# A transformer block on one core: a third value pair by Strassen, the exp and the statistics passes of a group moved, numerators in four row tiles, and the first loads from two queues

## The chip, the cores and the metric

The kernel runs on one core of a Trainium2 chip. The metric is the device time of one launch in microseconds (us), as the median of several executions. Each trace is of one execution.

Engine names are those of the profile: PE is TensorE's matmuls, PEld its weight loads, DVE is VectorE, ACT is ScalarE, POOL is GpSimd, SP is SyncE, which issues most DMAs.

## The reference, cut to what matters

```python
def reference(A_x, A_wqkv, A_wo, B_x, B_W_gate, B_W_up, B_W_down):   # S = 2048, D = 1024, H = 32, Dh = 32, F = 3584
    # A: linear attention on layernorm(x)
    qkv = layernorm(x) @ wqkv                        # q, k, v: 32 heads of 32
    phi = lambda t: where(t > 0, t + 1, exp(t)) + 1e-6
    kv  = einsum("bhsd,bhse->bhde", phi(k), v)       # one 32x32 block a head
    z   = einsum("bhsd->bhd", phi(k))
    o   = einsum("bhqd,bhde->bhqe", phi(q), kv) / (einsum("bhqd,bhd->bhq", phi(q), z) + 1e-6)
    h   = x + o @ wo
    # B: gated block on layernorm(h)
    out = h + (relu(g @ W_gate) * (g @ W_up)) @ W_down      # g = layernorm(h)
```

## The kernel before

The 2048 rows are 16 tiles of 128 rows, numbered from 0. The first stage goes through them in pairs (tiles 4 and 5 are the third pair), a group of key products and a group of value products for each pair; then come eight query groups, the output projection, and the gated block. A group is one level of Strassen's scheme: seven products of four 128x128x512 matmuls instead of eight. The order of the products is P1, P7, P6, P2, P5, P4, P3, and between them ScalarE copies a bank of PSUM, TensorE's output memory, into the next one (`fk1`, `fk2`), evacuates partial sums (`s7`, `sc`), and runs the exp of phi; VectorE adds and finishes phi. A hook is a place between two products where work of another stage is queued.

```python
def sgroup(...):                              # one group; hook(i) runs what other stages put there
    prod(a, X(0, 0), W(0, 0), True, "P1")
    ident_act(bank(b), bank(a), ..., "fk1")   # ScalarE; P6 waits for it
    hook(1)
    prod(f, SX(2), TW(2), True, "P7")         # SX: sums of x blocks (VectorE), TW: sums of weight blocks
    ident_act(s7, bank(f), ..., "s7")
    hook(2)
    prod(b, SX(1), TW(1), False, "P6")
    ident_act(bank(c), bank(b), ..., "fk2")   # P5 waits for it
    hook(3)
    prod(a, X(1, 0), W(1, 0), False, "P2"); ...; hook(4)
    prod(c, SX(0), TW(0), False, "P5")
    ident_act(sc, bank(c), ..., "sc"); s22 = ...; s22[0]()
    hook(5)
    prod(b, X(1, 1), TW(3), False, "P4"); s21 = ...; s21[0](); hook(6)
    prod(c, SX(3), W(1, 1), False, "P3")
    s12 = list(e12(...))
    if isq: s12.pop(0)()                      # exp; the other exps wait until hooks 1 to 3 of the next group
    pend[1], pend[2], pend[3] = s12, list(s22[1:]), list(s21[1:])
    hook(7)
```

The statistics of half of the tiles are made on ScalarE (a mean pass and a square pass over 1024 columns), in hooks 5 and 6 of a key group. The first two value pairs and the third (tiles 4 and 5) are plain products, `v_piece`, because x sums and weight sums come late at the start. The numerators take, for each tile, eight matmuls of 128 rows against a zero-padded kv block, which VectorE makes with a mask:

```python
    for g in range(NG):                                    # 8 groups of 4 heads
        mm(ps[:, nbk, c0:c0 + P + HPG], pqT[:, r, t, g, i * P:(i + 1) * P], kvz[:, g, 0:P + HPG], ...)   # 132 columns
```

A last part is how a normalised tile becomes a transposed one. VectorE normalises, SP issues a transposing DMA from SBUF to SBUF (`T1d`), and VectorE then makes the sums of x blocks (`x_sums`) that P7, P6, P5 and P3 of the groups of that pair need.

## Time and profile before

The time before is 747.6 us (747.31 to 748.15 in three executions). The first lines are from the page of the profile: its span, the busy time of each engine (share of the span, number of instructions), the DMA queue of PE's instruction fetches (packets, MB, share), and the shares of the chain of waits.

```profile
span 746.0 us, 10031 instructions
PE 736.1 (99%) x3539; PEld 336.0 (45%) x3595; DVE 536.7 (72%) x1071; ACT 309.7 (42%) x536; POOL 43.9 (6%) x90
...
q8 instruction: 28, 0.46, 0.3%
...
PE 88%; DVE 5%; ACT 4%; issue 2%; DMA 0%; SPq 0%; DVEq 0%; POOL 0%; ACTq 0%; POOLq 0%
```

TensorE is the limit. A reader should not take "99% busy" for "no loss", though: a 512-column matmul is drawn 379 ns long while the next one starts 216 ns after it, so a wait of 0.1 us hides under the overlap. Losses are read from the distance of starts.

The timeline of the kernel before, around the start of a value group (start, duration, engine, line, operation; `ps<-RW,RWG` at 57.95 is P7 and P6, four matmuls each, `RAB` P2, the next `RW,RWG` P5):

```profile
57.08 1.03 PE L616 MATMUL ps<-RAB 128*128 128x512 bf16 x4
57.22 1.06 ACT L659 ACTIVATE RXH<-RE 128x1024 bf16<-128x1024 bf16 x1
57.95 2.00 PE L616 MATMUL ps<-RW,RWG 128*128 128x512 f16 x8
58.27 0.58 ACT L621 ACTIVATE ps<-ps 128x512 f32<-128x512 f32 x1
59.78 1.03 PE L616 MATMUL ps<-RAB 128*128 128x512 bf16 x4
60.26 0.59 ACT L621 ACTIVATE ps<-ps 128x512 f32<-128x512 f32 x1
60.91 1.04 PE L616 MATMUL ps<-RW,RWG 128*128 128x512 f16 x4
```

P1 is issued at 57.08 and over by about 57.95, but its copy `fk1` starts at 58.27, behind the square pass of the statistics (57.22), and `fk2` at 60.26, behind two exps. P5 starts 1.13 us after P2 (60.91 less 59.78), where four matmuls need 0.86 us. A key-and-value pair takes 13.56 us and holds 0.48 us of such waits.

The numerators of one tile, between P4 and P3 of a query group:

```profile
149.51 1.03 PE L616 MATMUL ps<-RAB,RXH 128*128 128x512 bf16 x4
150.38 0.63 PE L616 MATMUL ps<-kvz,RAB 128*128 128x132 bf16 x8
150.85 1.02 PE L616 MATMUL ps<-RH,RO 128*128 128x512 f16 x4
```

Eight numerator matmuls take 0.47 us from start to start.

### The profile page before, as it was taken

The numbers are of one execution on the slowest core, as the hardware profiler recorded it, in microseconds if no ns is written. First come the engines' busy times: TensorE is split into PE (matmuls) and PEld (weight loads), VectorE is DVE, ScalarE is ACT, GpSimd is POOL, SyncE is SP. The second block draws the span as 40 slices with busy tenths as digits, with TensorE's granted clock in tenths as the row PEclk, the third lists the DMA queues.
The fourth block names the chain that finished last, engine by engine and source line by source line (L and its number), as shares of the span: only waits on it lengthen the run. The fifth ranks groups of instructions, "written<-read, shape, count | busy, mean of one in ns | idle before, by whom it ended". The sixth has DMA issues, their size and how long they took to land.

```text
span 746.0 us, 10031 instructions
## 1 busy us (share of the span) xinstructions
PE 736.1 (99%) x3539; PEld 336.0 (45%) x3595; DVE 536.7 (72%) x1071; ACT 309.7 (42%) x536; POOL 43.9 (6%) x90
## 2 busy tenths in 40 slices
PE   9999999999999999999999999999999999999998
PEld 4444444344554444444444444444444444444443
DVE  7788866898775899787877585766867677563343
ACT  4767656665832354544543100035444454520000
POOL 2411000001350000000000010000000000000000
PEclk9999999999999999999999999999999999999999
DMA  9642144023998797666428899742324242036764
GB/s 305 202 103 68 35 135 156 1 29 84 230 223 248 222 278 210 179 176 171 142 85 253 231 254 305 240 121 77 110 61 112 58 113 56 1 85 184 211 189 135
DMA packets 160226, 113.38 MB, mean 152 GB/s; under 512 B 51505, under 2 KB 141361, under 8 KB 160177
## 3 DMA queue, kind: packets, MB, share of 16 engines
q1 hardware_dynamic: 160176, 112.75, 54.1%
q8 instruction: 28, 0.46, 0.3%
q14 instruction: 22, 0.17, 0.1%
HBM read 85.46 MB, written 15.73 MB: 136 GB/s over the span
## 4 chain that ended last, share of the span: by engine, by line
PE 88%; DVE 5%; ACT 4%; issue 2%; DMA 0%; SPq 0%; DVEq 0%; POOL 0%; ACTq 0%; POOLq 0%
PE ps L616 88%; DVE RAB L691 1%; ACT ps L621 1%; ACT RX L684 1%; DVE RE L1058 1%; DVE RX L688 1%; ACT RXH L654 1%; ACT RXH L659 1%; ACT RX L621 1%; DVE RX L903 0%; DMA RW<-in_B_W_down_dram 0%; SPq L522 0%; DVE RXH L1082 0%; PE ps L748 0%; DVE RE L691 0%
## 5 line engine op out<-in xcount | busy, mean ns | idle before, releaser
L621 ACT ACTIVATE ps<-ps 128x512 f32<-128x512 f32 x154 | 89.8, 584 | 180.2 <-PE ps L616 161.5
L616 PE MATMUL ps<-RC,RO 128*128 128x512 f16 x672 | 154.4, 379 | 0.5 <-DVE RE L1239 0.4
L616 PE MATMUL ps<-RW,RAB 128*128 128x512 f16 (+1 forms) x681 | 150.1, 379 | 0.6
L616 PEld LDWEIGHTS ps<-RW,RAB 128*128 128x128 bf16 (+1 forms) x692 | 67.7, 98 | 81.6
L616 PE MATMUL ps<-RH,RWG 128*128 128x512 bf16 x435 | 103.2, 379 | 1.0 <-DVE RAB L1232 0.3
L621 ACT ACTIVATE RE<-ps 128x512 f32<-128x512 f32 x120 | 70.8, 597 | 75.3 <-PE ps L616 52.8
L616 PEld LDWEIGHTS ps<-RC,RO 128*128 128x128 f16 x672 | 65.5, 98 | 80.5 <-ACT ps L621 1.1
L616 PE MATMUL ps<-RC,RWG 128*128 128x512 f16 x320 | 76.6, 379 | 0.1
L616 PEld LDWEIGHTS ps<-RH,RWG 128*128 128x128 bf16 x448 | 43.8, 98 | 53.4 <-DVE RAB L1232 0.8
L1232 DVE TENSOR_TENSOR RAB<-ps,RAB 128x512 bf16<-128x512 f32 x28 | 19.3, 690 | 63.6 <-PE ps L616 63.6
L621 ACT ACTIVATE RAB<-ps 128x512 bf16<-128x512 f32 x56 | 33.4, 597 | 61.9 <-PE ps L616 61.8
L616 PE MATMUL ps<-RH,RO 128*128 128x512 bf16 (+1 forms) x242 | 58.3, 379 | 0.7
L616 PE MATMUL ps<-RW,RE 128*128 128x512 bf16 x248 | 56.8, 379 | 0.8 <-DVE RXH L1082 0.4
L616 PE MATMUL ps<-RAB 128*128 128x512 bf16 x196 | 47.7, 379 | 0.3
L616 PEld LDWEIGHTS ps<-RC,RWG 128*128 128x128 bf16 (+1 forms) x320 | 30.0, 98 | 39.9 <-ACT ps L621 5.9
L1163 DVE TENSOR_TENSOR RO<-RWG,RO 128x512 f16<-128x512 bf16 x108 | 45.4, 420 | 1.8
L1163 DVE TENSOR_TENSOR RO<-RWG 128x512 f16<-128x512 bf16 x108 | 40.7, 418 | 3.2 <-DMA RWG<-in_B_W_up_dram 1.6
L1239 DVE TENSOR_TENSOR RE<-ps,RE 128x512 f32<-128x512 f32 x56 | 38.3, 690 | 4.9 <-ACT RE L621 4.9
L1244 DVE TENSOR_TENSOR RE<-ps,RE 128x512 f32<-128x512 f32 x56 | 38.1, 681 | 0.0
L616 PEld LDWEIGHTS ps<-RH,RO 128*128 128x128 f16 (+1 forms) x256 | 24.6, 98 | 29.4 <-ACT RX L621 1.1
L616 PEld LDWEIGHTS ps<-RW,RE 128*128 128x128 bf16 x256 | 24.5, 98 | 27.9 <-DVE RXH L1082 0.7
L688 DVE TENSOR_SCALAR RX<-RX 128x512 bf16<-128x512 bf16 x64 | 18.6, 290 | 22.8 <-ACT RX L684 22.7
(118 smaller groups left out, 764.8 us busy)
## 6 DMA issues: line engine op xcount, KB each, us to landing
RWG<-in_B_W_gate_dram SPq DMA_DIRECT2D x28, 512.0 KB, 4.0
RWG<-in_B_W_up_dram SPq DMA_DIRECT2D x28, 512.0 KB, 5.1
RW<-t_scr SPq DMA_DIRECT2D x56, 256.0 KB, 3.3
RW<-in_B_W_down_dram SPq DMA_DIRECT2D x42, 256.0 KB, 4.0
RW<-in_B_W_down_dram SPq DMA_DIRECT2D x14, 512.0 KB, 4.1
t_scr<-RW SPq DMA_DIRECT2D x14, 512.0 KB, 5.0
RE<-in_A_x_dram SPq DMA_DIRECT2D x23, 256.0 KB, 3.2
RAB<-in_A_wqkv_dram SPq DMA_DIRECT2D x8, 512.0 KB, 8.0
```

Of the source, the lines that this page charges most:

```text
L616: lambda e: e.matmul(out_ap, lhsT, rhs, start=start, stop=stop, skip_group_check=skip),
L621: PL.add("act", lambda e: e.activation(out=dst, in_=src, func=func), reads=reads, writes=writes, name=name)
L654: PL.add("act", lambda e: e.activation(out=junk, in_=src, func=ACTF.Identity, scale=1.0 / D, accum_out=sv[:, 0:1]), reads=src_bufs, writes ...
L659: PL.add("act", lambda e: e.activation(out=junk, in_=src, func=ACTF.Square, scale=float(D) ** -0.5, accum_out=sv[:, 1:2]), reads=src_bufs, ...
L684: PL.add("act", lambda e: e.activation(out=Et[:, k, :], in_=src, func=ACTF.Exp), reads=[src_buf], writes=[B_E[k]], name=name + "_exp")
L688: PL.add("dve", lambda e: e.tensor_scalar(out=Et[:, k, :], in0=Et[:, k, :], scalar1=1.0, scalar2=1e-6, op0=ALU.min, op1=ALU.add), reads=[] ...
L691: PL.add("dve", lambda e: e.scalar_tensor_tensor(out=dst_ap, in0=src, scalar=C1, in1=Et[:, k, :], op0=ALU.add, op1=ALU.max), reads=[src_bu ...
L1058: PL.add("dve", lambda e: e.tensor_tensor(out=osb[:, k, :].rearrange("p (g h e) -> p g h e", h=HPG, e=Dh), in0=nv[:, :, 0:P].rearrange("p ...
L1163: PL.add(eng, lambda e: e.tensor_tensor(out=Tring[:, k, j], in0=in0, in1=in1, op=ALU.subtract), reads=reads, writes=[B_T[k][j]], name="T%d ...
L1232: PL.add("dve", lambda e: e.tensor_tensor(out=hh[:, f1, 0:SBW], in0=bank(BA[1]), in1=r11[:, rr, :], op=ALU.mult), reads=[B_bank[BA[1]], B_ ...
L1239: PL.add("dve", lambda e, w=w: e.tensor_tensor(out=ftmp[:, 4 + w, :], in0=bank(BF_[w]), in1=ftmp[:, 2 + w, :], op=ALU.add), reads=[B_bank[ ...
L1244: PL.add("dve", lambda e, w=w: e.tensor_tensor(out=ftmp[:, 6 + w, :], in0=bank(BB[w]), in1=ftmp[:, w, :], op=ALU.add), reads=[B_bank[BB[w] ...
```

## The change

Its intent is to fill the last bubbles of the first 233 us: (1) the third value pair also by Strassen, 28 matmuls for 32; (2) at the end of a group one exp goes before P3's evacuation and one before the next group's `fk1`, and the square pass is cut in two halves placed between other work; (3) numerators of 32 rows x 33 columns, four row tiles of the array at once (a row tile is a band of 32 of TensorE's 128 rows, one for each head of a group; it is not one of the 16 tiles of x), so that the kv blocks need no zero padding and no masks (ten small ScalarE copies bring them from PSUM); (4) the first x tile and the first weights from two DMA queues. The core of the diff:

```diff
-        if isq:
+        for f_ in s22[1:2]:            # before P3: the exp of the P5 result
+            f_()
+        prod(c, SX(3), W(1, 1), False, "P3")
+        s12 = list(e12(bank(c), B_bank[c]))
+        if isphi:
             s12.pop(0)()
-        pend[1] = s12
-        pend[2] = list(s22[1:])
-        pend[3] = list(s21[1:])
+        pend[1] = list(s22[2:]) + s12 + list(s21[1:])
 ...
-        v_piece(4, 0, lambda: run_pend(1))
-        v_piece(4, 1, lambda: run_pend(3))      # and v_piece(5, 0), v_piece(5, 1)
+        v_group(p + 2, {2: v2, 3: v3, 5: v5, 6: v6})      # for p = 0 as for all others
 ...
-            if 3 <= p + 2 < NP_:                # hook 6
-                x_sums(p + 2)
+            if p + 2 < NP_:                     # hook 5: one sum, hook 6: the other three
+                x_sums(p + 2, 0)
 ...
+                for h in range(HPG):            # numerators
+                    sl = slice(h * Dh, (h + 1) * Dh)
+                    mm(ps[:, NB[h], g * NUW:g * NUW + Dh + 1], pqT[sl, r, t, g, i * P:(i + 1) * P],
+                       kvz[sl, g, 0:Dh + 1], ...)
 ...
+                if r == 0 and ct >= 1:          # ten ScalarE copies of the kv blocks
+                    for h_ in (1, 3, 4, 7):
+                        if kvc:
+                            hooks[h_] = kvc.pop(0)
 ...
-                dma(..., writes=[B_x1[i][c]])                        # first x tile, two halves
+                dma(..., writes=[B_x1[i][c]], eng=("sp", "act")[c])
```

## The prediction

> **What bounds the kernel.** TensorE: the page gives PE 736.1 us busy of a 746.0 us span, and 88% of the chain of waits. The gated block (from about 233 us) is untouched, so all happens before. The timeline of PE shows 512-column matmuls starting 0.216 us apart, eight 132-column numerator matmuls in 0.47 us (150.38 to 150.85), sixteen 129-column ones in 0.94 us. From 8.26 to 233.3 us there are 940 of 512 columns (202.8 us), 256 short ones (15 us) and three transposed tiles (1.4 us): 219 us of 225. So some 6 us of bubbles, and 8.3 us before the first projection matmul.
>
> **Terms.**
>
> 1. Third value pair: 32 matmuls become 28. Minus 4 x 0.216 = 0.9 us, all on the chain.
>
> 2. Group boundaries. Each steady key-and-value pair (50.24 to 63.80, 13.56 us) holds about 0.48 us of waits: 0.26 and 0.10 us in the value group, 0.03 to 0.05 elsewhere. The timeline shows ScalarE running the mean and square passes (1.06 us each plus 0.19) just before the value group's bank copies (58.27, 60.26), so P6 waits. Halving the square pass between copies, and putting a group's first exp (0.6 us) inside the last product, removes the queue. Such waits: 3.2 us in the key/value part, 1.9 us in the eight query groups (0.15 to 0.26 before P4). I expect half to go: minus 2.5 us.
>
> 3. Numerators. Per token tile eight matmuls of 128 rows x 132 columns become 32 of 32 rows x 33 columns. Today 16 x 0.47 = 7.5 us, all on PE's chain. If four row tiles stream together, 8 x 33 columns take about 0.3 us: minus 2.7 us. But weight loads go from 8 to 32; the Trainium skill, "TensorE: Matmul & The Clock Gate" (LDWEIGHTS; back-to-back), says that a load costs by columns, not rows, and that starts are at least about 25 ns apart; "TensorEngine Tiling (Array Packing)", key properties, that a change of mode drains the array. 32 pairs at 25 to 30 ns plus two drains would be about 1 us: plus 8 us. This trace shows only pairs at 58 ns. I take minus 1 us, leaning to a gain.
>
> 4. Start. Removing the masks frees 1.1 us of VectorE (2.05 to 3.34), and x lands earlier (VectorE waited 0.45 us at 7.68). But the first transposes (6.46) follow twelve dummy matmuls that end about then: minus 0.2 us.
>
> 5. Masking on VectorE (1.9 us, 139.57 to 141.2) becomes ten ScalarE copies (estimate 0.3 us each) in query groups where ScalarE is 65% busy: neutral. Accumulation one hook later removes the 0.25 us wait at 116.56.
>
> **Sum.** 747.6 - 0.9 - 2.5 - 1 - 0.2 - 0.2 = 742.8; say 742.5 us, 8 in 10 within 738.0 to 748.0. Faster by over 2% 0.02, within 2% 0.95, slower 0.03.
>
> **What would show it.** 1: PE records 28 matmuls for that pair. 2: a steady pair's period falls from 13.56 to about 13.2 us, ScalarE's copy starting right after P1. 3: the numerator stretch between output-projection tiles falls below 0.47 us, the period from 3.92. 4: first transpose still at about 6.4 us. From the gated block on, the timelines are shifted copies.
>
> **What would make it wrong.** Row tiles limited by issue or weight loads; the earlier value group stalling on VectorE's weight sums (80% busy in 0 to 40 us); ScalarE's ten copies delaying bank copies.

## The result, and the profile after

The changed kernel takes 746.06 us (745.83 to 748.27 in four executions) against 747.74 us; the ratio is 0.9984 with a 95% interval of 0.9964 to 1.0004. In later rounds the unaltered repeat gave 746.78 against 747.90 us, ratio 0.9985 (0.9973 to 0.9997); the first interval includes no change at all, the second doesn't. So the gain is 1.1 to 1.7 us, a third or less of the 5.1 us that were predicted.

The same lines of the page of the changed kernel:

```profile
span 744.1 us, 10780 instructions
PE 731.3 (98%) x3914; PEld 330.4 (44%) x3975; DVE 534.4 (72%) x1064; ACT 316.2 (42%) x558; POOL 42.4 (6%) x93
...
q8 instruction: 31, 0.51, 0.3%
...
PE 85%; DVE 7%; issue 3%; DMA 2%; ACT 2%; SPq 1%; POOL 0%; DVEq 0%; ACTq 0%
```

PE's share of the chain fell from 88% to 85%, and DMA rose from 0% to 2%. (61 matmul records are missing from this profile; in that of the repeat, where none is, PE has 87% and DMA 2%.) The 384 additional numerator matmuls also make PE's program longer: 31 fetch packets of 16 KB instead of 28. (For the 7134 and 7889 instructions that the profiles record on PE and PEld, the packets come to 64 bytes an instruction in both kernels, so this queue is taken to be PE's.)

The same place of a value group:

```profile
57.04 1.03 PE L595 MATMUL ps<-RAB 128*128 128x512 bf16 x4
57.90 1.93 PE L595 MATMUL ps<-RW,RWG 128*128 128x512 f16 x8
58.16 0.58 ACT L600 ACTIVATE ps<-ps 128x512 f32<-128x512 f32 x1 [0.16 <-PE ps L595]
59.67 1.03 PE L595 MATMUL ps<-RAB 128*128 128x512 bf16 x4
60.53 1.03 PE L595 MATMUL ps<-RW,RWG 128*128 128x512 f16 x4
```

ScalarE now waits for PE before `fk1`, and P5 follows P2 after 0.86 us. This part of the change does what it should. The numerators:

```profile
148.61 1.03 PE L595 MATMUL ps<-RAB,RXH 128*128 128x512 bf16 x4
149.57 0.37 PE L595 MATMUL ps<-kvz,RAB 32*128 32x33 bf16 x32
149.88 1.04 PE L595 MATMUL ps<-RH,RO 128*128 128x512 f16 x4
```

32 matmuls take 0.31 us from the first start to the next product, against 0.47 for the eight; 0.10 us of the gain is lost in front of them: the first comes 0.96 us after P4's first (149.57 less 148.61), where it was 0.87. This entry cost is 95 to 96 ns in all 16 tiles. In the trace the four matmuls of four row tiles start 2 to 5 ns apart, and those of one and the same row tile 25 ns apart (the second 40 ns after the first). The product behind them starts 104 ns after the last; before the change it was 60 ns.

Then where did the rest go? The table cuts the span at the first matmul of P4 of each key group (k0 to k7) and query group (q0 to q7), read from the timeline of PE. A single missing record can shift a start by 0.22 us. (In the time before the gated block, "pair" is a key group and a value group.)

| stretch, us | before | changed | changed, repeat |
|---|---|---|---|
| start to k0 | 27.77 | 27.73 | 28.04 |
| k0 to k1 (third value pair) | 13.97 | 14.42 | 13.99 |
| k1 to k2 | 13.56 | 13.16 | 13.15 |
| k2 to k3 | 13.55 | 13.16 | 13.15 |
| k3 to k4 | 13.56 | 14.34 | 14.50 |
| k4 to k6 | 27.03 | 26.35 | 26.35 |
| k6 to q0 | 13.95 | 13.22 | 13.22 |
| q0 to q4 (first query half) | 26.12 | 26.23 | 26.22 |
| q4 to q7 (with numerators) | 20.14 | 19.59 | 19.59 |
| q7 to the gated block | 63.63 | 63.23 | 63.43 |
| gated block to the end | 512.73 | 512.66 | 512.69 |

Four pairs gained 0.3 to 0.4 us each, as predicted, and so did the end of the key groups and the second query half. Three places gave it back: the third value pair, which needs four matmuls less but no less time; the pair k3 to k4, 0.8 to 0.9 us longer; and the first query half. The third value pair in the changed kernel (its P7 and its P6):

```profile
30.32 1.04 PE L595 MATMUL ps<-RW,RWG 128*128 128x512 f16 x4
31.80 1.02 PE L595 MATMUL ps<-RW,RWG 128*128 128x512 f16 x4 [0.44 <-DVE RWG L816]
```

P6 comes 0.61 us late and waits for VectorE's sums of x (line 816). In the repeat it is only 0.18 us late, and behind ScalarE's copy. The worst place in the timeline of PE of the changed kernel (`RAB` is P1 of the sixth value pair, the first `RW,RWG` its P7, the second its P6):

```profile
70.19 1.03 PE L595 MATMUL ps<-RAB 128*128 128x512 bf16 x4
71.67 1.04 PE L595 MATMUL ps<-RW,RWG 128*128 128x512 f16 x4 [0.45 <-DVE RWG L816]
73.15 1.02 PE L595 MATMUL ps<-RW,RWG 128*128 128x512 f16 x4 [0.45 <-DVE RWG L816]
```

P7 and P6 each come 0.61 us late and wait for the sums of x. In the kernel before, P7, P6 and P2 of the same pair follow with 0.1 us of waits in all:

```profile
70.64 1.03 PE L616 MATMUL ps<-RAB 128*128 128x512 bf16 x4
71.50 2.00 PE L616 MATMUL ps<-RW,RWG 128*128 128x512 f16 x8
73.34 1.03 PE L616 MATMUL ps<-RAB 128*128 128x512 bf16 x4
```

The chain of waits of that stretch (start, length, what) shows what the sums waited for:

```profile
65.95 5.21 DMA RAB<-RXH
...
71.18 0.43 DVE RWG L816
```

The transposed load of tile 11 took 5.21 us. The one before it (64.05) landed in 3.06 us, and tile 11's in the kernel before in 3.51 us. The view of DMA in the stretch 68.3 to 69.4 us (queue, packets, MB, share of the engines), in the changed kernel:

```profile
q1 hardware_dynamic: 67, 0.02, 74.2%
q8 instruction: 1, 0.02, 5.3%
```

and in the kernel before, whose fetch came at 64.1 us:

```profile
q1 hardware_dynamic: 987, 0.30, 129.8%
```

In the middle of the load one 16 KB packet of instructions arrives (68.39 to 69.32 in the trace), and while it is under way the loads hardly move. The standstill is longer than the packet: from 68.55 to 69.95 us the data packets that end in any 0.2 us of the trace hold at most 2 KB together, where the kernel before has 29 to 71 KB at the same place of its load.

### The profile page after: what moved, and what is told of

It reads as the page before. It is cut to its first block, busy times and chain, and to the rows that moved or that the text cites. A ratio compares the mean times of both kernels' runs of the same rounds, so it can differ in the third digit from the quotient of the medians.

```text
span 744.1 us, 10780 instructions
## 1 busy us (share of the span) xinstructions
PE 731.3 (98%) x3914; PEld 330.4 (44%) x3975; DVE 534.4 (72%) x1064; ACT 316.2 (42%) x558; POOL 42.4 (6%) x93
## 4 chain that ended last, share of the span: by engine, by line
PE 85%; DVE 7%; issue 3%; DMA 2%; ACT 2%; SPq 1%; POOL 0%; DVEq 0%; ACTq 0%
PE ps L595 85%; SPq L501 1%; DVE RAB L681 1%; DMA RE<-in_A_x_dram 1%; DVE RE L1056 1%; DVE RX L678 1%; DMA RAB<-RXH 1%; DVE RX L897 1%; ACT RX L674 1%; ACT RXH L633 0%; DVE RWG L816 0%; DMA RW<-in_B_W_down_dram 0%; DVE RW L791 0%; ACT ps L600 0%; DVE RXH L1080 0%
## 5 line engine op out<-in xcount | busy, mean ns | idle before, releaser
L595 PE MATMUL ps<-RH,RWG 128*128 128x512 bf16 x448 | 106.0, 379 | 0.2 <-DVE RAB L1230 0.2
L600 ACT ACTIVATE RAB<-ps 128x512 bf16<-128x512 f32 x56 | 33.4, 597 | 61.9 <-PE ps L595 61.8
L595 PE MATMUL ps<-RH,RO 128*128 128x512 bf16 (+1 forms) x228 | 55.5, 379 | 1.5
L595 PE MATMUL ps<-RAB 128*128 128x512 bf16 x172 | 42.5, 379 | 0.3
L609 DVE BATCH_NORM_STATS2 st<-RE 128x6 f32<-128x512 bf16 x34 | 22.1, 683 | 16.4 <-DMA RE<-h_scr 12.5
```

Of the source, the lines that this page charges most:

```text
L595: lambda e: e.matmul(out_ap, lhsT, rhs, start=start, stop=stop, skip_group_check=skip),
L600: PL.add("act", lambda e: e.activation(out=dst, in_=src, func=func), reads=reads, writes=writes, name=name)
L609: PL.add("dve", lambda e: e.bn_stats(out=st6[:, k, c * 6:(c + 1) * 6], in_=src_full[:, c * BCH:(c + 1) * BCH]), reads=[src_chunk_bufs[c]], ...
```

## The experiments

The theory: the local gains are real, and new waits eat them, each with its own cause: (A) at k3 to k4 the position of PE's instruction fetch, which meets a transposed load; (B) at the third value pair VectorE and ScalarE, which can't deliver so early; (C) in the first query half the ten ScalarE copies in front of bank copies. The rivals: the order of VectorE's sums makes them late by itself; the row tiles are the loss; the third pair is worth its 0.9 us and the loss is elsewhere. Twelve kernels ran. All gave correct results. Ratios are against the kernel before in the same rounds.

| run | edit | median us | ratio (95%) | profiled span |
|---|---|---|---|---|
| a1_repeat | changed kernel, unaltered | 746.78 | 0.9985 (0.9973 to 0.9997) | 744.3 |
| a2_shift | dummies cut finer | 745.38 | 0.9966 (0.9954 to 0.9978) | 744.0 |
| a3_nums128 | numerators as before | 745.99 | 0.9972 (0.9961 to 0.9984) | 744.2 |
| a4_pieces | third value pair as before | 744.72 | 0.9970 (0.9956 to 0.9984) | 743.0 |
| b1_slots | 4 statistics slots | 745.92 | 0.9971 (0.9957 to 0.9986) | 745.0 |
| b2_copies5 | kv copies in one gap | 745.75 | 0.9970 (0.9957 to 0.9983) | 744.1 |
| b3_oneq | loads from one queue | 747.09 | 0.9990 (0.9977 to 1.0003) | 745.3 |
| b4_all | all repairs | 743.56 | 0.9940 (0.9927 to 0.9953) | 740.7 |
| c1_best | and copies in three groups | 743.02 | 0.9940 (0.9928 to 0.9953) | 742.2 |
| c2_best128 | repaired, numerators as before | 743.70 | 0.9946 (0.9933 to 0.9960) | 742.2 |
| c3_before_wt | before, one repair alone | 746.30 | 0.9983 (0.9971 to 0.9996) | 744.6 |
| c4_before_shift | before, dummies cut finer | 748.56 | 1.0016 (1.0003 to 1.0029) | 746.6 |

### The changed kernel again

No edit.

> The changed kernel unaltered. Theory: its loss is built in, so the profile again has the wait of about 0.6 us each at two products of the sixth value pair (near 71.7 and 73.2 us), because the transposed load of tile 11 lands 5.2 us after issue instead of 3.0 to 3.7 with one 16 KB instruction-fetch packet inside it; the first transposes start at 6.5 to 6.8 us and VectorE's first statistics again begin at 3.7 us, later than 3.26 before. Time 745.6 to 746.4. Rival: the 5.2 us landing was an accident of one execution; then the wait is gone here and the profiled span is about 743 us.

Measured: tile 11's load took 5.37 us with the fetch packet at 68.4 us again, and P7 and P6 of the sixth value pair were late by 0.77 and 0.61 us. The span was 744.3 us, not 743. The median of 746.78 is above the expected range, the profiled execution (746.10) is in it. The late load is no accident of one execution. The first statistics began at 3.60 us, and the first transposes at 6.68.

### The same work, PE's program shifted

```diff
-        pe_dummies(12, P1_POOL)
+        pe_dummies(32, P1_POOL, 192)      # 32 x 192 = 12 x 512 columns, 40 instructions more
```

> The same work, but the 12 start-up dummy matmuls of 512 columns are 32 of 192 (6144 columns both), which puts 40 more instructions in front and moves every later PE instruction fetch some 4.3 us earlier against the program. Theory (fetch collides with tile 11's transposed load): fetches move from 46.4, 68.4, 90.4 to about 42, 64, 86, where the kernel before had them; tile 11 lands in about 3.5 us, the two waits of 0.6 us go, and the time falls by 1.2 us to about 744.8. Rival (the waits come from splitting the x sums and moving them one hook earlier): they stay, time as the repeat within 0.3.

Measured: the fetch came at 63.1 us, tile 11's load took 3.54 us, and both waits are gone. The timeline of PE at the same place:

```profile
70.42 1.03 PE L595 MATMUL ps<-RAB 128*128 128x512 bf16 x4
71.28 1.93 PE L595 MATMUL ps<-RW,RWG 128*128 128x512 f16 x8
73.05 1.03 PE L595 MATMUL ps<-RAB 128*128 128x512 bf16 x4
```

k3 to k4 fell from 14.50 to 13.15 us, and the median is 1.4 us under the repeat's. Nothing was changed but the cut of the dummies, and so the number of instructions in front, so the order of VectorE's sums is not by itself what makes them late; the rival falls. (The profiled span gained only 0.3 us: this execution lost 0.98 us at 19.0 us to a late load of x and 1.2 us at 244.6, of which below; the repeat lost 0.4 us at each.) All later runs agree. In the 14 profiles there are 168 transposed loads of the first stage. In ten of them a 16 KB fetch packet arrives later than 1.3 us after issue (it starts at 2.05 to 2.84 us), and these ten took 4.46 to 5.61 us; the other 158 took 3.03 to 3.76 us. The limit of 1.3 us was drawn after the fact: in seven of the 158 a packet lay earlier than that, and they took 3.03 to 3.24 us. This is shown for the first stage alone. Later on, with other traffic, transposed loads took up to 4.98 us in the kernel before with no such packet in them.

### The numerators as before

```diff
-            mm(ps[:, NB[h], ...], pqT[sl, r, t, g, ...], kvz[sl, g, 0:Dh + 1], ...)      # 32 x (32 rows, 33 columns)
+            mm(ps[:, nbk, c0:c0 + P + HPG], pqT[:, r, t, g, ...], kvz[:, g, 0:P + HPG], ...)   # 8 x (128 rows, 132 columns)
+   # and masks, padding on VectorE, no ScalarE copies, as in the kernel before
```

> The changed kernel with the numerators as before: 8 matmuls of 128 rows x 132 columns a tile, masks and zero-padded kv made on VectorE, no ScalarE copies. Theory: a numerator stretch costs 0.47 us of PE again against 0.31 plus 0.095 of entry wait, 0.065 a tile, 1.0 us in all; the query groups of the first half lose the ScalarE copies' waits (0.8 us of waits before P4 and P2 become 0.3 to 0.5); net plus 0.3 to 0.8 us. Rival: row tiles are the loss (double rate of instruction fetches from 150 us on, late transposed loads), then this is faster than the repeat by 0.5 us or more.

Measured: the period of a query group with numerators is 6.59 instead of 6.53 us, so the row tiles are worth 0.06 us a tile, as expected. But the first query half took 25.58 us (q0 to q4) instead of 26.22, so the copies that row tiles need cost 0.64 us there. And in the output projection, where twelve tiles should have gained some 0.8 us, the stretch from q7 to the gated block is 63.47 against 63.43 us. In all the spans are alike (744.2 and 744.3); the median is even 0.8 us lower, which the traces don't show. The expectation of a slower kernel failed: as the change has them, row tiles gain nothing. By its median the run meets the rival's condition (faster by 0.5 us), but not for the rival's reason: tile 11 landed late here too (5.58 us), and what was regained is the copies' 0.64 us.

### The third value pair as before

```diff
+            if p == 0:
+                v_piece(4, 0, mid0); sq.pop(0)(); v_piece(4, 1); ...; v_piece(5, 0); ...; v_piece(5, 1)
+                x_sums(2); kvaccs(0)
+            elif p + 2 < NP_:
```

> The changed kernel with the third value pair made by 32 plain matmuls in four pieces, as before, its sums later. Theory: the 0.86 us that Strassen saves there is given back by waits of P6 on VectorE's sums (0.61 us at 31.80) and on ScalarE (0.20 us at 33.73), so the stretch between the first products P7 of key groups 0 and 1 stays at 13.9 us and the time is that of the repeat within 0.4 us. Rival: Strassen of this pair is worth its 0.9 us and the loss sits only elsewhere, then this is slower by 0.9 us.

Measured: k0 to k1 took 13.89 us against 13.99, with four more matmuls, so Strassen of this pair saved nothing. The whole was 2.1 us faster than the repeat, which neither theory had said; the trace shows why: the different program moved the fetch from 68.4 to 63.9 us, tile 11 landed in 3.58 us, and k3 to k4 was 13.15 us. That is a second kernel in which the stall goes with the fetch.

### Four slots for the row statistics

```diff
-        s1 = sb("s1", [P, 2, 4], f32)
+        s1 = sb("s1", [P, 4, 4], f32)
-            k = len(ln1_a) % 2
+            k = len(ln1_a) % 4
```

> The changed kernel with four instead of two slots for ScalarE's row statistics, nothing else. Theory: at 39.4 us the product P6 of key group 1 waits 0.47 to 0.52 us because ScalarE's mean pass for tile 9 needs the slot of tile 6, whose normalisation stands behind the x sums in VectorE's queue; with more slots the pass starts before 36.4 us, the wait goes and key group 0 to key group 1 (from P4 to P4) falls from 14.0 to 13.5 us; the late landing of tile 11 and the 1.4 us at 71.7 and 73.2 stay, as the PE stream is the same. Time about 0.4 us under the repeat. Rival (the wait is of ScalarE's load itself): the passes run at about the same time and the wait stays above 0.3 us.

In the changed kernel the mean pass for tile 9 waits for VectorE (engine idle 1.61 us before it, released by the normalisation in line 723), and so P6 of key group 1 comes late:

```profile
37.06 1.06 ACT L633 ACTIVATE RXH<-RE 128x1024 bf16<-128x1024 bf16 x1 [1.61 <-DVE RXH L723]
...
38.12 1.03 PE L595 MATMUL ps<-RC,RWG 128*128 128x512 f16 x4
39.51 1.04 PE L595 MATMUL ps<-RC,RWG 128*128 128x512 f16 x4 [0.36 <-ACT ps L600]
```

With four slots:

```profile
35.66 1.05 ACT L633 ACTIVATE RXH<-RE 128x1024 bf16<-128x1024 bf16 x1
...
38.43 1.93 PE L595 MATMUL ps<-RC,RWG 128*128 128x512 f16 x8
```

The wait is gone, and k0 to k1 fell to 13.55 us, as the theory said. So half of what Strassen saves at this pair was lost to a reuse of a slot, not to ScalarE's load. The other half is, by the trace, ScalarE's queue: P5 of the third value pair comes 0.38 us late (34.03) because `fk2` (33.38) stands behind half a square pass (32.77), and that is nearly all of the 0.40 us between 13.55 and a steady pair's 13.15. The median is 0.9 us under the repeat's, but the profiled span is longer, because of waits at other places (0.52 us at 25.8, 0.74 at 225.5, the late tile 11 again).

### The copies in ScalarE's idle gap

```diff
-                    for h_ in (1, 3, 4, 7):
-                        if kvc:
-                            hooks[h_] = kvc.pop(0)
+                    hooks[5] = lambda fs=[kvc.pop(0) for _ in range(n_)]: [f_() for f_ in fs]     # 2, 2, 3, 3
```

> The changed kernel with its ten ScalarE copies of the kv blocks all at one place of a group, between the P5 evacuation and the exp that follows it, where ScalarE idles 0.76 us for VectorE's add (2, 2, 3, 3 copies in four groups). Theory: where the copies stand in front of a bank copy they delay it, 0.8 us in all; here the P4-to-P4 times of query groups 1 to 2 and 2 to 3 fall from 6.47 and 6.51 to 6.13 to 6.2 us, as in the run without the copies, and the time falls by 0.6 us. Rival (ScalarE simply has no room): the waits move to other products and the sum of the groups stays.

In the changed kernel a copy (`kvz`) stands before `fk1`, and P6 at 133.33 comes 1.09 us after P7, 0.23 us late:

```profile
132.24 1.03 PE L595 MATMUL ps<-RWG,RX 128*128 128x512 f16 x4
132.34 0.32 ACT L600 ACTIVATE kvz<-ps 32x192 bf16<-32x192 f32 x1
132.69 0.58 ACT L600 ACTIVATE ps<-ps 128x512 f32<-128x512 f32 x1
133.33 1.04 PE L595 MATMUL ps<-RWG,RH 128*128 128x512 f16 x4
```

With the copies behind the P5 evacuation two of them fit in the gap before the exp:

```profile
130.41 0.65 ACT L600 ACTIVATE kvz<-ps 32x192 bf16<-32x192 f32 x2
131.28 0.63 ACT L674 ACTIVATE RX<-RX 128x512 bf16<-128x512 f32 x1 [0.22 <-DVE RX L897]
```

q1 to q2 and q2 to q3 fell from 6.47 and 6.51 to 6.14 us, as expected. But the last three copies stood before the first numerators, and q4 to q5 rose from 6.53 to 7.11 us. That was a mistake of this edit, mended below.

### The first loads from one queue

```diff
-                    ..., eng=("sp", "act")[c])
+                    ..., eng="sp")
-        load_wkv(2, half=0, eng="act")
-        act_warm()
+        act_warm()
+        load_wkv(2, half=0)
```

> The changed kernel with all first loads from one queue, in the order of before. Theory: from two queues the two halves of the first x tile share the DMA engines and land together at 3.3 to 3.9 us; from one queue the first half lands at 2.9 us as before (there the masks held VectorE until 3.26), so the first statistics start at about 2.9 us, normalisation is ready about 0.6 us earlier, and the first transposes start at about 6.0 us if the dummies end by then, first projection at about 7.5 us instead of 8.1; time 0.3 to 0.6 us less. Rival: the queues don't matter, first statistics again at 3.3 to 3.7 us.

Measured: the first half of the first x tile landed at 2.90 us instead of 3.57 to 3.67 in the changed kernel and its repeat, and statistics began at 2.92.

So two queues do delay the first half by 0.7 us, and 0.2 to 0.3 us of it reach PE: with two queues (changed kernel and repeat) PE sits idle until the tile is normalised and starts the first transposes at 6.79 and 6.68 us, with one the tile was ready at 5.86 us and they start behind the last dummy matmul, at 6.46. Then later loads of x came late (k0 at 28.70 us), and the kernel was not faster, so the expected 0.3 to 0.6 us did not show. The order of the first loads is at most a small part of the loss.

### All repairs

```diff
   # four slots, copies in hook 5, one queue, dummies 32 x 192, and:
-        m5, q5 = ln1_stats_act(5); m5()          # before the transposes of tile 3
+        # after them, as in the kernel before
-        wt_at = {0: [0], 1: [1, 2], 2: [3, 4]}   # sums of the down weights, by gated pair
+        wt_at = {1: [0, 1], 2: [2, 3], 3: [4, 5]}
```

> All repairs together: four slots, copies in ScalarE's idle place, one queue, the dummies as 32 of 192 columns (moves the instruction fetches off tile 11's load), the statistics of tile 5 again behind the transpose copies of tile 3, and the sums of the down weights begun one pair later, so that VectorE does not block on their load at 240 to 244 us (a wait of 0.4 to 1.4 us of PE at 244.7). Theory: waits of 0.5 + 0.7 + 0.5 + 1.3 + 0.4 + 0.5 us are gone, time 742.0 to 743.5 us. Rival: most of these waits are not what limits and come back in other places; time 744.5 us or more.

Measured: 743.56 us, just over the expected range, and 740.7 us in the profiled execution, which took 742.42. k0 to k1 13.55, k3 to k4 13.15, q1 to q3 12.28 us; the late copies cost their 0.58 us. The first five gated pairs took 60.43 instead of 61.8 us, with no wait left.

### Copies in three groups

```diff
-   n_ = 2, 2, 3, 3 copies in groups (0, 1), (0, 2), (0, 3), (1, 0)
+   3, 3, 4 copies in groups (0, 1), (0, 2), (0, 3)
```

> All repairs, with the ten kv copies in three groups (3, 3, 4) of the first query half instead of four; in the run before, the three copies in the last group stood in front of the first numerators and cost 0.58 us (7.11 instead of 6.53 us from query group 4 to 5). Theory: that goes and nothing else changes: profiled span 740.1 us, time about 743.0 us. Rival: four copies in one gap overfill it, 0.3 us come back in query group 3.

Measured: 743.02 us, the best median, ratio 0.9940 as the run before. The profiled span was 742.2 us, not 740.1. q4 to q5 is 6.53 us again, and query group 3 did not grow (6.17). The profiled execution took 743.92, the slowest of its five, and shows the same lottery in a new place. Here it is tile 7's load (issued at 39.74, 5.37 us) that met the fetch, at 42.1 us, and the fourth value pair waited 0.83 us; in the profiled execution of the run before, the fetch came at 42.4 us, just after that load had landed. Also k0 came 1.1 us later here (29.25), after a wait for x. Late loads of x at the start are thus a second source of scatter: in the profiles of the changed kernel and its variants k0 lies between 27.73 and 29.25 us. The spread of this kernel's five executions (742.14 to 743.92) has the size of such events; that it is made of them is not shown, as only one execution was profiled.

### Numerators as before, in the repaired kernel

The edit is that of a3_nums128, on the repaired kernel.

> The repaired kernel with the numerators as 8 full-height matmuls a tile, masks and padding on VectorE. It tells what row tiles are worth once their copies wait for nothing. Theory: 0.065 us a tile, so query periods 6.59 instead of 6.53 us, and in all 0.5 to 1.0 us slower than the repaired kernel. Rival: row tiles are worth nothing or less: within 0.2 us or faster.

Measured: 743.70 against 743.02 us. Query periods are 6.59 and 6.53 us, and from q1 to the gated block it takes 101.73 against 101.16 us. Both profiles have tile 7's late load, so they may be compared. Row tiles are worth 0.6 us, once their copies hold nothing up. The gain in single executions (742.14 to 743.92 against 742.94 to 744.01) is within their spread.

### Two controls on the kernel before

The gated block goes through its 3584 columns in 14 steps of two 128-column tiles, the gated pairs. The first control takes the one repair that has nothing to do with the change:

```diff
-        wt_at = {0: [0], 1: [1, 2], 2: [3, 4]}
+        wt_at = {1: [0, 1], 2: [2, 3], 3: [4, 5]}
```

> A control: the kernel before, with only the sums of the down weights begun one pair later, the one repair that has nothing to do with the change. Before has waits of 0.46, 0.52, 0.07 and 0.33 us in the first gated pair (246.7 to 251.1 us), as the changed kernel has. Theory: they go, 1.4 us, and the time is 746.4 us; so 1.4 of the 4.2 us of the repaired kernel belong to this and not to the change. Rival: the blocked load only moves, time within 0.4 us of before.

Measured: 746.30 against 747.51 us, and the first five gated pairs 60.43 us. So 1.2 to 1.4 of the repaired kernel's 4.5 us come from here. VectorE had stood still for 4.2 us before these sums, with later work behind them.

The second cuts the dummies finer, to move a fetch into tile 11's load:

```diff
-        pe_dummies(12, P1_POOL)
+        pe_dummies(115, P1_POOL, 53)
```

> A converse test on the kernel before: its 12 dummies of 512 columns as 115 of 53, 206 instructions more in front, so that the instruction fetch of about 90.6 us comes some 22 us earlier, at about 68.4 us, into tile 11's transposed load (issued 66.3, landed 69.8). Theory: the load then lands after about 5.3 us, at 71.6, and the sixth value pair waits 0.5 to 1.3 us for its sums, in a kernel without any part of the change; the time rises by 0.5 to 1.3 us, if the start is the same. Rival: only the changed order of VectorE makes that load late; it lands in 3.5 us.

Measured: the aim failed. The fetches came at 27.6, 49.6 and 73.8 us, and tile 11 landed in 3.54 us. But tile 5's load, issued at 24.89 us, met the fetch at 27.6 and took 5.52 us (3.69 in the kernel before), and no wait of PE followed, because its sums are needed later. So a fetch lengthens a transposed load in the kernel before, too; that it would cost PE time there at tile 11 was not shown. The 1.1 us more in the median come from the start (a wait of 0.67 us at 11.8, k0 at 28.28 instead of 27.77) and waits at 247 us, as far as one profile tells; that they fall into the expected 0.5 to 1.3 us is chance.

## Why the prediction was right or wrong

The prediction was 742.5 us with a range of 738.0 to 748.0; measured were 746.06 and, in later rounds, 746.78. The time is in the range and "within 2%" was right, but the change was put at minus 5.1 us and is minus 1.1 to 1.7.

The step that failed is the one from local savings to the sum: each saving was taken to stay on the chain, and the moved work to be free. By the repeat's trace the third pair gained 0.0 us instead of 0.9, the pair k3 to k4 lost 0.9 us where the other pairs gained 0.4, the copies cost 0.6 us instead of nothing, and the start lost 0.3 us instead of gaining 0.2. Together that is 0.9 + 1.3 + 0.6 + 0.5 = 3.3 us, and by the profiled spans (746.0 and 744.3 us) 3.4 of the 5.1 us are missing. (The numerators brought 0.6 us less than expected as well, but more waits went elsewhere than the half that was expected.) Point by point:

1. **"Minus 4 x 0.216 = 0.9 us, all on the chain."** Wrong. The 28 matmuls are there, but k0 to k1 is 13.99 to 14.42 us where it was 13.97. The pair, moved forward, waits for VectorE's sums (0.61 us at 31.8 in the first profile) and for ScalarE (0.20 and 0.52 us at 33.7 and 39.5). In the repeat, ScalarE alone makes three products late, by 0.18, 0.24 and 0.47 us (at 31.7, 33.6 and 39.4), which is all that Strassen saves. The prediction named VectorE's weight sums as a risk and gave it no number; what came late were the sums of x, in one of the two profiles, and ScalarE's copies, which it did not name here. The run with four slots shows that 0.42 us of the 0.86 can be had.
2. **"I expect half to go: minus 2.5 us."** The mechanism was right, and where nothing else interfered more than half went: the period fell from 13.56 to 13.15 us ("about 13.2"), which is 0.41 of a pair's 0.48 us of waits, and k1 to k3, k4 to q0 and q4 to q7 together gained 2.8 us (0.8, 1.4 and 0.55, the last with the numerators' share). What failed is the step from a removed wait to the sum. PE's position in time moved against everything that doesn't run at PE's pace, and one transposed load met an instruction fetch: 1.2 to 1.4 us of new waits in k3 to k4, 0.8 to 0.9 net.
3. **"I take minus 1 us" for the numerators.** This was a hedge between minus 2.7 us and the estimate of plus 8 us from a page's figure, and that PE's own time per tile came out at it is luck: 0.31 + 0.10 against 0.47 us is 0.065 a tile, 1.0 us in 16. The figure of the Trainium skill ("TensorE: Matmul & The Clock Gate") that starts are at least about 25 ns apart does not hold between row tiles here (2 to 5 ns), only within one row tile (25 ns). What takes more than half of the gain back fits what "TensorEngine Tiling (Array Packing)", key properties, says: a change of tiling mode drains the array. 95 ns more in front and 104 ns behind are measured; that the drain is their cause was not tested. As a net gain the term was too large: in the output projection 0 to 0.4 of 0.8 us arrived. Part of the rest is a wait for VectorE there, which grew from 0.55 us (180.24 before) to 0.81 us (178.82).
4. **Start, minus 0.2 us.** Wrong: k0 came 0.04 us earlier in one profile and 0.27 us later in the other. The first half of x landed 0.7 us later, not earlier, and the first transposes, put at "about 6.4", came at 6.79 and 6.68 us, behind the normalised tile and no longer behind the dummies.
5. **Copies "neutral".** Wrong by 0.6 us. ScalarE has room on average (the prediction put it at 65% busy), but the copies stood in front of bank copies that PE waits for. In the right gap they are free.
6. **"From the gated block on, the timelines are shifted copies."** Right (512.73 and 512.66 to 512.69 us). It hid that this block began with 1.4 us of waits, worth as much as the change.

The prediction should have asked, of each place that PE reaches earlier, what it will wait for there. Two of its three stated worries came true, without a number: a stall of the earlier value group (though not on weight sums) and the copies in front of bank copies. "Row tiles limited by issue", the one it dwelt on, did not. The meeting of a load with an instruction fetch was not foreseen.

## What to carry to other kernels

When the limiting engine is 99% busy, each bubble removed moves its whole later timeline against the DMAs and the other engines, so cost a change by the next release at every place that it makes earlier, not by the sum of removed waits. Look in the trace for loads that take half as long again as their fellows and see what else moved in that time; a few instructions more or less in front moved the result by 1.4 us here, as much as the change itself. Small work for an engine with an average of 35% to spare belongs in a gap where nothing that the limiting engine waits for stands behind it.

The version that beats both kernels is the changed one with the repairs (743.02 us, ratio 0.9940, so 4.5 us under the kernel before); 1.2 to 1.4 us of that are open to the kernel before as well.

## What the Trainium skill lacked or had wrong

- "Runtime: NRT & Kernel Launch", section on instruction fetch mechanics, says that instructions come in blocks of 16 KiB (256 instructions) and that crossing a block boundary costs one queue update, "mostly hidden". The block size agrees (28 packets for 7134 recorded instructions, 31 for 7889, or 7950 in the repeat, where no record is missing). It lacks that the transfer itself gets in the way of other DMAs: in the first stage a transposing load with such a packet in its data part took 4.46 to 5.61 us (10 of 168), the others 3.03 to 3.76 us, and this cost PE 0.8 to 1.6 us where the load was needed at once. Why all of the load stands still for 1.4 us while one packet of 0.9 us goes by was not found.
- "TensorE: Matmul & The Clock Gate", on back-to-back starts: "never drops below ≈25 ns however small N is". Between matmuls in four different row tiles, each with its own weight load, starts are 2 to 5 ns apart. Within one row tile they are 25 ns apart (the second 40 ns), so the sentence holds tile by tile and not for the engine. Its own section on row tiling (starts about 4 ns apart) is the one that agrees.
- "TensorEngine Tiling (Array Packing)" says that a change of mode drains the array and gives no number. Here entering 32-row tiles after a 512-column matmul cost 95 ns beyond the usual 216, and the next full-height matmul started 104 ns after the last small one. For 32 matmuls of 33 columns the entry alone is more than half of the saving (0.47 to 0.31 us).
- "DMA: Bandwidth & Descriptors" says that DMAs issued from several engines interleave on the same 16 DMA engines. It lacks what that costs the part that is needed first: with a first load split over two queues that half landed at 3.29 to 3.67 us (seven profiles), from one queue at 2.86 to 3.15 (seven), and the second half there at 3.40 to 3.66.
